# Token product of two batches by seven block products, and the last weights rounded from the pair before the last

## The chip, the cores and the metric

The kernel runs on one core of one Trainium2 chip. The metric is the device time of one execution in microseconds (us). The core's engines run side by side, each with its own queue in order: TensorE (PE) does matrix products out of SBUF into PSUM, VectorE (DVE), ScalarE (ACT) and GpSimd (POOL) do elementwise work, and SyncE (SP) issues the DMA transfers.

## The reference

Two blocks follow each other. The first is an attention in which each query sees only the keys that fall to the same of 16 clusters; the second is a mixer: a small network across the tokens, then one across the channels.

```python
# B, H, S, D = 4, 8, 768, 64; 16 clusters
q_assign = argmax(q_n @ c_n.T); k_assign = argmax(k_n @ c_n.T)     # by batch and head
scores = where(q_assign[:, None] == k_assign[None, :], q @ k.T / 8, -1e9)
x = softmax(scores) @ v                            # bridged to x: (4, 768, 512)

h = relu(x.T @ w_tok1) @ w_tok2                    # 768 -> 256 -> 768 tokens
u = x + h.T
out = u + relu(u @ w_ch1) @ w_ch2                  # 512 -> 1536 -> 512 channels
```

The inputs are random; q, k and v are float32, and the four weights arrive as float64, so the kernel has to round them to float32 itself.

## The kernel before

**Attention.** The loop over `g` runs over 16 pairs of heads (4 batches x 4 pairs). `scores(g, qh)` makes two score tiles per key block, ScalarE takes exponentials (L423), `add_up` sums them on VectorE (L431), `values` multiplies by v (L441), and ScalarE copies the result out (L448). A DMA transpose brings it to token order (`pair_turn`), ScalarE puts it into x (`pair_put`, L466), and VectorE divides by the sums (`pair_out`, L492). Routing for pair g+2 goes beside that.

**Rounding the weights.** `weight_steps` yields one step per piece of at most 512 columns. A step finishes piece i-2 (`rest`: three VectorE operations at L210, L215 and L220, then an integer add on GpSimd at L227), does the ScalarE part of piece i-1 (L203 and L205) and issues the load of piece i on SyncE (L197, 512 KB). The call `rounding(n)` puts n steps at that place of the program order. The first three weights (19 pieces) go into pairs 0 to 14, one or two steps a pair. `w_ch2` (12 pieces) takes the space of the routing tiles and starts in pair 15.

**Token stage.** `tok1(b, t)` is one tile of relu(x^T w_tok1): six accumulated matmuls of 128x512 (L521), and a relu, by turns on VectorE and ScalarE. `tok2(b, j)` is one row block of the second product: two matmuls (L530), and one VectorE add into x (L533). The list `ends` orders them: tok1 of batch b+1 goes ahead of tok2 of batch b. Between them go the rest of the rounding, the sums of the first channel weights (`left_weights`, four VectorE operations over all columns), and `u_steps(0)`, which turns u of batch 0: a ScalarE copy (L591), a DMA transpose (L593) and a ScalarE copy back (L604) for each of eight pieces. `u_sums` then makes four sums of u on VectorE (L544).

**Channel stage.** Both channel products already work with seven block products instead of eight (Strassen in Winograd's form). `chunk` does one chunk of a product in three PSUM tiles X, Z and Y: X takes A11 B11, then S2 T2, S3 T3 and A22 T4 on top; Z takes S1 T1, then S4 B22; Y takes A12 B21. After each product VectorE or ScalarE reads what is in PSUM and adds it to one or another block of the result, while TensorE goes on in another tile. The last product of a chunk is put behind the first one of the next (`late`). The S are sums of the left blocks, the T sums of the right ones. `right_weights` makes the sums of `w_ch2` in the first two chunks.

All engines work in program order; there is no scheduler, the order is as written. PSUM holds eight banks: in the attention six for scores and two for `ps_av`; afterwards two buffers each of X, Z and Y in `ps_m`, and `ps_av`, hardly used.

Of the kernel before, what the change touches and what calls it, by code (L numbers as in the profile page):

```python
# [8 lines left out]
F32 = mybir.dt.float32  # L9
# [10 lines left out]
P = 128  # L20
# [28 lines left out]
def kernel(  # L49
# [131 lines left out]
    def weight_steps(pool, W, names):  # L181
# [8 lines left out]
        def tmp(name, dt, n):  # L190
            bufs = 1 if name == "wT" else 2
            return pool.tile([P, WMAX], dt, tag=name, name=name, bufs=bufs)[:, 0:n]

        def load_bits(src, p):
            n = p["n"] = src.shape[1]
            raw = pool.tile([P, WMAX, 2], U32, tag="raw", name="raw", bufs=3)[:, 0:n]
            nc.sync.dma_start(raw.rearrange("p n two -> p (n two)"), src.bitcast(U32))  # L197
            p["lo"], p["hi"] = raw[:, :, 0], raw[:, :, 1]

        def scalar_part(p):  # L200

            p["h"] = tmp("wh", U32, p["n"])
            nc.scalar.activation(out=p["h"].bitcast(F32), in_=p["hi"].bitcast(F32), func=ACT.Abs)  # L203
            p["up"] = tmp("wup", I32, p["n"])
            nc.scalar.activation(out=p["up"], in_=p["lo"], func=ACT.Copy, scale=float(2.0**-29))  # L205

        def rest(dst, p):
# [11 lines left out]
            T = tmp("wT", U32, p["n"])  # L219
            nc.vector.scalar_tensor_tensor(  # L220
                out=T, in0=p["hi"], scalar=0xC0000000, in1=h,
                op0=ALU.bitwise_and, op1=ALU.bitwise_or,
            )
            T, up = T.bitcast(I32), p["up"]
            if len(dst.shape) == 3:
                T, up = (y.rearrange("t (p j) -> t p j", j=NJ) for y in (T, up))
            nc.gpsimd.tensor_tensor(out=dst.bitcast(I32), in0=T, in1=up, op=ALU.add)  # L227
# [3 lines left out]
        for i in range(len(pieces) + 2):  # L231

            def step(i=i):
                if 2 <= i:
                    rest(pieces[i - 2][0], parts[i - 2])
                if 1 <= i <= len(pieces):
                    scalar_part(parts[i - 1])
                if i < len(pieces):
                    load_bits(pieces[i][1], parts[i])

            yield step
# [259 lines left out]
    turns = [0, 0]  # L501

    def relu(dst, src):
        turns[0] += 1
        if turns[0] % 2:
            nc.vector.tensor_scalar_max(out=dst, in0=src, scalar1=0.0)
        else:
            nc.scalar.activation(out=dst, in_=src, func=ACT.Relu)

    def mtile(shape, name):  # L510
        turns[1] += 1
        return pools["ps_m"].tile(shape, F32, tag="XZ"[turns[1] % 2], name=name)
# [3 lines left out]
    def tok1(b, t):  # L516
# [8 lines left out]
        relu(h1s[b][:, t], pf)  # L525

    def tok2(b, j):
        pu = mtile([P, DM], "pu")
        for t in range(NT):
            nc.tensor.matmul(  # L530
                pu, lhsT=W["tok2"][:, t, j], rhs=h1s[b][:, t], start=(t == 0), stop=(t == NT - 1)
            )
        nc.vector.tensor_tensor(out=xs[b][:, j], in0=pu, in1=xs[b][:, j], op=ALU.add)  # L533
# [12 lines left out]
    def add(dst, a, b):  # L546
        nc.vector.tensor_tensor(out=dst, in0=a, in1=b, op=ALU.add)  # L547

    def left_weights():
# [3 lines left out]
        A = {  # L553
# [6 lines left out]
        yield lambda: add(A["S1"], A["A21"], A["A22"])  # L560
        yield lambda: sub(A["S2"], A["S1"], A["A11"])
        yield lambda: sub(A["A21"], A["A11"], A["A21"])
        yield lambda: sub(A["S4"], A["A12"], A["S2"])
        A["S3"] = A["A21"]
        pools["A"] = A

    def right_weights():

        w = W["ch2"]
        B_ = {  # L570
            f"B{i + 1}{j + 1}": w[:, 6 * i : 6 * i + 6, 256 * j : 256 * j + 256]
            for i in range(2)
            for j in range(2)
        }
        extra = pools["wsums"].tile([P, 3, NCT // 2, DM // 2], F32, name="w2s")
        B_["T1"], B_["T2"], B_["T4"] = (extra[:, i] for i in range(3))
        yield lambda: sub(B_["T1"], B_["B12"], B_["B11"])
        yield lambda: sub(B_["T2"], B_["B22"], B_["T1"])
        yield lambda: sub(B_["B12"], B_["B12"], B_["B22"])
        yield lambda: sub(B_["T4"], B_["B21"], B_["T2"])  # L580
        B_["T3"] = B_["B12"]
        pools["B"] = B_
# [31 lines left out]
    def u_sums():  # L614
        uT = pools["uT"]
        uTs = pools["uTs"] = pools["u"].tile([P, 3, NF // 2, HS], F32, name="uTs")
        R = {"B11": uT[:, 0, 0:2], "B21": uT[:, 0, 2:4], "B22": uT[:, 1, 2:4]}
        R["T1"], R["T2"], R["T4"] = (uTs[:, i] for i in range(3))
        R["T3"] = b12 = uT[:, 1, 0:2]
        sub(R["T1"], b12, R["B11"])  # L620
        sub(R["T2"], R["B22"], R["T1"])
        sub(R["T3"], R["B22"], b12)
        sub(R["T4"], R["B21"], R["T2"])
        pools["R"] = R
# [3 lines left out]
    def chunk(n, product, done, last=False):  # L628


        def ptile(tag):
            return pools["ps_m"].tile([P, n], F32, tag=tag, name="p" + tag)

        X = ptile("X")
# [4 lines left out]
        Z = ptile("Z")  # L639
        product(Z, "S1", "T1", True)  # L640
        done("p5", Z)
        Y = ptile("Y")
# [25 lines left out]
        late.append(end)  # L668

    def ch1_chunk(part, i):  # L670
# [47 lines left out]
        chunk(HS, product, done)  # L718
# [114 lines left out]
    ends = [lambda t=t: tok1(0, t) for t in range(NT)]  # L833
    for b in range(B):
        if b + 1 < B:
            ends += [lambda b=b, t=t: tok1(b + 1, t) for t in range(NT)]
        ends += [lambda b=b, j=j: tok2(b, j) for j in range(NJ)]

# [10 lines left out]
    for g in range(NPAIR):  # L849
        final = g == NPAIR - 1  # L850
        if final:
            assert not weights
            routing.close()
            W["ch2"] = pool("wc2pool", 1, side="right").tile([P, NCT, DM], F32, name="wc2")
            weights = list(weight_steps(stage, W, ("ch2",)))
# [17 lines left out]
        rounding(1)  # L873
        for qh in range(2):
            values(g, qh)
# [11 lines left out]
        rounding(final or g % 2 == 0 and 0 < g < EARLY)  # L887

    ps_sc_stack.close()
    pools["ps_m"] = pool("ps_m", 2, space=PSUM)  # L890
    for m in range(9):
        ends.pop(0)()
        if m == 1:
            pair_put(NPAIR - 1)
            pair_out(NPAIR - 1)
        if m % 3 == 2:
            rounding(2)
    assert not state
    attention.close()
    pools["wsums"] = pool("wsums", 1, side="right")  # L900
    pools["u"] = pool("upool", 1, side="right")
    beside = weights + list(left_weights())
    turning = list(u_steps(0))
    while ends:
        for _ in range(-(-len(beside) // len(ends))):
            beside.pop(0)()
        ends.pop(0)()
        if len(ends) < 18 and turning:
            turning.pop(0)()
    u_sums()  # L910
    staging.close()
    tokens.close()
    pools["mlp"] = pool("mlp", 1)
    beside = list(right_weights())
    for b in range(B):
        for part in range(2):
            for i in range(3):
                ch1_chunk(part, i)
# [5 lines left out]
                for _ in range(2):  # L924
                    if beside:
                        beside.pop(0)()
# [10 lines left out]
            if part == 1 and b + 1 < B:  # L937
                u_sums()
# [217 lines left out]
```

## Time and profile before

| | |
|---|---|
| median of three runs | 844.19 us (844.08 to 844.33) |
| span of the profiled execution | 842.8 us, that run took 844.64 us |
| attention | to 317.7 us |
| token stage | 317.7 to 401.3 us |
| channel stage | from 401.3 us |

The page gives for each engine how long it was busy; in the list of groups a row is one kind of instruction: line, engine, operation, output and inputs, shapes, count, then busy time in all and the mean of one in ns, then how long the engine idled just before such instructions and on whom it waited. In a timeline a row has the start, the length, the instruction, and in brackets the idle time before it and who ended it. Starts are from the beginning of the span. The engine that the end depends on is found in the chain of work that ended last. Records of TensorE overlap: its pace is read from starts.

### The profile page before, as it was taken

What the parts mean: (1) busy time and instruction counts of PE and PEld (TensorE: products, weight loads), DVE (VectorE), ACT (ScalarE), POOL (GpSimd) and SP (SyncE); (2) the same over time, 40 slices, a digit from 0 to 9 for tenths busy, and PEclk for the clock granted to TensorE, in tenths of its full rate; (3) what the DMA queues carried; (4) which work ended last, traced back from release to release, by engine and by line L of the source; (5) the groups of instructions that cost most, each with busy time, mean ns of one, the idle gap of its engine ahead of it and who ended that gap; (6) DMA issues with size and microseconds to landing.
All of it is one profiled execution on the core that took longest, in us unless ns stands there. A gap on an engine that the chain in (4) does not pass through costs nothing.

```text
span 842.8 us, 10776 instructions
## 1 busy us (share of the span) xinstructions
PE 833.5 (99%) x4099; PEld 507.2 (60%) x4099; DVE 501.5 (60%) x846; ACT 374.9 (44%) x571; POOL 45.6 (5%) x40
## 2 busy tenths in 40 slices
PE   9999999999999999999999999999999999999997
PEld 4444444445444444444577686785876867768676
DVE  6879898989898862893653434423454333443342
ACT  5678677777777762453210352103612035220210
POOL 1001010101101000330000000000000000000000
PEclk9999999999999999999999999999999999999999
DMA  8887566867775312541000050000310012200001
GB/s 152 149 162 140 114 138 139 162 131 156 148 136 120 57 44 73 169 99 29 0 1 1 19 107 26 0 1 19 88 45 0 1 19 47 85 1 0 1 16 64
DMA packets 183963, 60.19 MB, mean 71 GB/s; under 512 B 172768, under 2 KB 176864, under 8 KB 183904
## 3 DMA queue, kind: packets, MB, share of 16 engines
q1 hardware_dynamic: 182304, 59.04, 33.3%
q8 instruction: 34, 0.56, 0.3%
q10 hardware_dynamic: 1600, 0.39, 0.2%
q14 instruction: 25, 0.20, 0.1%
HBM read 34.64 MB, written 6.29 MB: 49 GB/s over the span
## 4 chain that ended last, share of the span: by engine, by line
PE 90%; DVE 7%; issue 1%; ACT 0%; DMA 0%; SPq 0%; POOL 0%; DVEq 0%; POOLq 0%
PE sc L416 17%; PE pX L734 15%; PE pX L683 15%; PE av L441 12%; PE pZ L683 7%; PE pZ L734 7%; PE ph L521 4%; PE pY L734 4%; PE pY L683 4%; PE pu L530 3%; DVE sum L431 1%; PE small L477 1%; DVE wh L215 1%; DVE wT L220 1%; PE small L301 1%; DVE wh L210 1%
## 5 line engine op out<-in xcount | busy, mean ns | idle before, releaser
L423 ACT ACTIVATE ex<-sc 128x768 f32<-128x768 f32 x192 | 148.9, 810 | 27.0 <-PE sc L416 15.4
L416 PE MATMUL sc<-qkT 64*128 64x384 f32 x768 | 155.1, 482 | 0.0
L431 DVE TENSOR_TENSOR sum<-sum,ex 128x768 f32<-128x768 f32 x128 | 127.7, 998 | 27.4 <-ACT ex L423 14.7
L441 PE MATMUL av<-ex,va 128*64 128x384 f32 x768 | 127.4, 488 | 0.0
L441 PEld LDWEIGHTS av<-ex,va 128*64 128x64 f32 x768 | 53.8, 137 | 71.7 <-issue 69.0
L416 PEld LDWEIGHTS sc<-qkT 64*128 64x128 f32 x768 | 68.5, 187 | 36.1 <-issue 35.2
L691 ACT COPY p<-pX 128x384 f32<-128x384 f32 x24 | 11.4, 475 | 139.1 <-PE pX L683 120.7
L683 PE MATMUL pX<-uT,wc 128*128 128x384 f32 x192 | 67.4, 487 | 0.0
L416 PE MATMUL sc<-ohT 64*128 64x384 bf16 x384 | 63.3, 324 | 0.3 <-DVE sim L317 0.2
L683 PEld LDWEIGHTS pX<-uT,wc 128*128 128x128 f32 x192 | 36.2, 190 | 24.7 <-issue 1.0
L448 ACT COPY avrows<-av 128x768 uint16<-128x768 uint16 x32 | 25.5, 796 | 47.1 <-PE av L441 47.1
L227 POOL TENSOR_TENSOR wc<-wT,wup 128x512 int32<-128x512 int32 x24 | 33.0, 1375 | 191.4 <-DVE wT L220 191.4
L604 ACT COPY uT<-ucols 128x768 uint16<-128x768 uint16 x32 | 33.7, 1052 | 20.3 <-DMA ucols<-urows 20.3
L521 PE MATMUL ph<-x,wt 128*128 128x512 f32 x96 | 41.9, 594 | 0.8 <-DVE x L533 0.8
L416 PEld LDWEIGHTS <-ohT 64*128 64x128 bf16 x384 | 20.3, 94 | 35.7 <-issue 11.1
L530 PE MATMUL pu<-h,wt 128*128 128x512 f32 x96 | 41.7, 592 | 0.0
L547 DVE TENSOR_TENSOR c<-pZ,u 128x384 f32<-128x384 f32 x24 | 13.4, 558 | 46.8 <-PE pZ L683 46.8
L702 ACT ACTIVATE hA<-hA 128x384 f32<-128x384 f32 x24 | 12.6, 523 | 63.4 <-DVE hA L547 63.4
L547 DVE TENSOR_TENSOR x<-pX,x 128x256 f32<-128x256 f32 x24 | 10.2, 423 | 42.8 <-PE pX L734 42.8
L683 PE MATMUL pZ<-uTs,w1s 128*128 128x384 f32 x96 | 35.0, 487 | 0.4 <-DVE uTs L544 0.4
L734 PE MATMUL pX<-wc,hA 128*128 128x256 f32 x144 | 35.0, 379 | 0.0
L734 PE MATMUL pZ<-w2s,hS 128*128 128x256 f32 x144 | 35.0, 379 | 0.0
(121 smaller groups left out, 1224.0 us busy)
## 6 DMA issues: line engine op xcount, KB each, us to landing
raw<-in_moe_w_ch_dram SPq DMA_DIRECT2D x24, 512.0 KB, 4.3
va<-in_v_dram SPq DMA_DIRECT2D x16, 384.0 KB, 3.7
out_dram<-x SPq DMA_DIRECT2D x24, 256.0 KB, 2.2
qk<-in_k_dram SPq DMA_DIRECT2D x60, 96.0 KB, 3.8
qk<-in_q_dram SPq DMA_DIRECT2D x60, 96.0 KB, 3.4
raw<-in_moe_w_tok_dram SPq DMA_DIRECT2D x3, 512.0 KB, 4.3
raw<-in_moe_w_tok_dram SPq DMA_DIRECT2D x4, 384.0 KB, 3.9
ucols<-urows SPq DMA_TRANSPOSE x32, 2.8
```

The lines of the kernel that those rows point to most:

```text
L227: nc.gpsimd.tensor_tensor(out=dst.bitcast(I32), in0=T, in1=up, op=ALU.add)
L416: nc.tensor.matmul(sc[:, h, 0:HS], lhsT=src[rows, 1, j], rhs=src[rows, 0, js], start=start, stop=not start,)
L423: nc.scalar.activation(out=ex, in_=sc[:, :, 0:HS], func=ACT.Exp, scale=SM_SCALE)
L431: nc.vector.tensor_tensor(out=acc, in0=acc if j > 1 else st["ex", qh, 0], in1=st["ex", qh, j], op=ALU.add)
L441: nc.tensor.matmul(av[h * D : (h + 1) * D], lhsT=st["va"][:, h, j], rhs=ex[:, h], start=(j == 0), stop=(j == NJ - 1),)
L448: nc.scalar.copy(out=st["rows"][:, qh], in_=av.bitcast(U16).rearrange("p (t w) -> p w t", w=2))
L521: nc.tensor.matmul(pf, lhsT=W["tok1"][:, j, t * P : (t + 1) * P], rhs=xs[b][:, j], start=(j == 0), stop=(j == NJ - 1),)
L530: nc.tensor.matmul(pu, lhsT=W["tok2"][:, t, j], rhs=h1s[b][:, t], start=(t == 0), stop=(t == NT - 1))
L547: nc.vector.tensor_tensor(out=dst, in0=a, in1=b, op=ALU.add)
L604: nc.scalar.copy(out=out, in_=pools.pop(("ucols", i)).rearrange("p w j t -> p w (j t)"))
L683: nc.tensor.matmul(psum, lhsT=A[a][:, k, c * P : (c + 1) * P], rhs=R[r][:, k], start=start and k == 0, stop=k == 1, skip_group_check=not s ...
L734: nc.tensor.matmul(psum, lhsT=h2[a][:, k, i * P : (i + 1) * P], rhs=Bw[w][:, 3 * part + k], start=start and k == 0, stop=k == 2, skip_grou ...
```

## The change

The second token product takes two batches at once, side by side as the columns of the right operand, and is made from seven block products. The left operand is `w_tok2` in 2 x 2 blocks (two halves of the hidden index, two halves of the token blocks), the right one the relu tiles `h1s` of batches b and b+1. Each block has three chunks; `tok2_chunks` takes them by turns, three X, three Z and two Y banks at a time, and adds what stands in each bank straight into x after each product, so that an intermediate sum in a bank is added wherever it belongs. `token_weights` and `token_sums` make the S and T. The order is now tok1 of two batches, then 21 products, then the same for the other two.

PSUM: `ps_m` has three buffers each of X and Z; Y takes the two banks of `ps_av`, in the channel stage too. All relus of tok1 go to ScalarE.

Rounding: `rest` works in place in `wh`, the ScalarE part writes over the low words in `raw`, and raw has four buffers and wh three. For `w_ch2` the steps begin in pair 14, load two steps ahead of the ScalarE part (`ahead=2`), and add on VectorE instead of GpSimd. The sums of the first channel weights are made by chunks of 128 columns: chunk 0 in the token stage, chunk c after chunk c-1 of batch 0. Those of the second are made in halves, one for each part of batch 0. `u_sums` comes in two halves, around the last of the token product.

```diff
-    def weight_steps(pool, W, names):
+    def weight_steps(pool, W, names, ahead=1, adder=nc.gpsimd):
...
-            p["up"] = tmp("wup", I32, p["n"])
+            p["up"] = p["lo"].bitcast(I32)
...
-            nc.gpsimd.tensor_tensor(out=dst.bitcast(I32), in0=T, in1=up, op=ALU.add)
+            adder.tensor_tensor(out=dst.bitcast(I32), in0=T, in1=up, op=ALU.add)
...
-        for i in range(len(pieces) + 2):
+        for i in range(len(pieces) + ahead + 1):
...
-    def tok2(b, j):
-        pu = mtile([P, DM], "pu")
-        for t in range(NT):
-            nc.tensor.matmul(
-                pu, lhsT=W["tok2"][:, t, j], rhs=h1s[b][:, t], start=(t == 0), stop=(t == NT - 1)
-            )
-        nc.vector.tensor_tensor(out=xs[b][:, j], in0=pu, in1=xs[b][:, j], op=ALU.add)
...
+    def left_chunk(c):
+        return left_sums(pools["A"], lambda x: x[:, :, c * P : (c + 1) * P])
...
+    def token_sums(b, t):
...
+        if t == 0:
+            sub(R["T1"], R["B12"], R["B11"])
+        else:
+            sub(R["T2"], R["B22"], R["T1"])
+            sub(R["T3"], R["B22"], R["B12"])
+            sub(R["T4"], R["B21"], R["T2"])
...
+    def tok2_chunks(b, half):
...
+        kinds = {
+            "p1": ("X", "A11", "B11", "c11"),
+            "p5": ("Z", "S1", "T1", "c22"),
+            "c11": ("Y", "A12", "B21", "c11"),
+            "u2": ("X", "S2", "T2", "c12"),
+            "c12": ("Z", "S4", "B22", "c12"),
+            "c22": ("X", "S3", "T3", "c22"),
+            "c21": ("X", "A22", "T4", "c21"),
+        }
+
+        def product(name, i):
+            tag, a, r, to = kinds[name]
+            start = name in ("p1", "p5", "c11")
+            if start:
+                banks[tag, i] = ptile(tag, DM)
+            nc.tensor.matmul(
+                banks[tag, i], lhsT=A[a][:, i], rhs=R[r], start=start, stop=True,
+                skip_group_check=not start,
+            )
+            x = xs[b + int(to[2]) - 1][:, HJ * (int(to[1]) - 1) + i]
+            add(x, banks[tag, i], x)
+
+        orders = (
+            (("p1", "012"), ("p5", "012"), ("c11", "01"), ("u2", "012"), ("c12", "01")),
+            (("c22", "012"), ("c12", "2"), ("c11", "2"), ("c21", "012")),
+        )
...
+        if g == NPAIR - 2:
+            assert not weights
+            routing.close()
+            W["ch2"] = pool("wc2pool", 1, side="right").tile([P, NCT, DM], F32, name="wc2")
+            weights = list(weight_steps(stage, W, ("ch2",), 2, nc.vector))
+            rounding(1)
+        rounding(g == NPAIR - 1)
...
+    for b in (0, 2):
+        tok1(b, 0)
+        if b == 0:
+            take(weights, 1)
+            pair_put(NPAIR - 1)
+            pair_out(NPAIR - 1)
...
+            take(list(token_weights()), 4)
+        else:
+            take(turning, 2)
+            take(weights, 2)
+        tok1(b, 1)
+        take(weights, 2)
+        if b == 2:
+            take(turning, 2)
+        tok1(b + 1, 0)
+        token_sums(b, 0)
+        take(weights, len(weights) if b == 2 else 1)
+        if b == 2:
+            left_weights()
+            take(list(left_chunk(0)), 4)
+        tok1(b + 1, 1)
+        token_sums(b, 1)
+        if b == 2:
+            take(turning, len(turning))
+        tok2_chunks(b, 0)
+        if b == 2:
+            u_sums(0)
+        tok2_chunks(b, 1)
+        if b == 0:
+            turning = list(u_steps(0))
...
+                if b == 0:
+                    c = 3 * part + i + 1
+                    for sums_of in left_chunk(c) if c < NCT // 2 else ():
+                        sums_of()
+                    take(others, min(len(others), 2))
```

## The prediction

> **What bounds the kernel now.** I read the page's busy table and 40 slices first, then the chain that ended last, then the groups by form, and last the timelines of TensorE, VectorE, ScalarE and SyncE from 280 to 432 us, where the change acts.
>
> ```profile
> span 842.8 us, 10776 instructions
> ...
> PE 833.5 (99%) x4099; PEld 507.2 (60%) x4099; DVE 501.5 (60%) x846; ACT 374.9 (44%) x571; POOL 45.6 (5%) x40
> ...
> PE   9999999999999999999999999999999999999997
> ...
> DVE  6879898989898862893653434423454333443342
> ...
> PE 90%; DVE 7%; issue 1%; ACT 0%; DMA 0%; SPq 0%; POOL 0%; DVEq 0%; POOLq 0%
> ```
>
> TensorE has work in every slice and holds 90% of the chain. VectorE is near full in the attention (slices 0 to 12) and again in 16 and 17 (337 to 379 us, the token products). A gain has to take TensorE instructions away, or gaps between them. TensorE's timeline of the token stage and its end:
>
> ```profile
> 317.72 20.87 PE L521 MATMUL ph<-x,wt 128*128 128x512 f32 x48
> 338.42 10.46 PE L530 MATMUL pu<-h,wt 128*128 128x512 f32 x24
> 348.72 10.46 PE L521 MATMUL ph<-x,wt 128*128 128x512 f32 x24
> 359.02 10.46 PE L530 MATMUL pu<-h,wt 128*128 128x512 f32 x24
> 370.24 10.57 PE L521 MATMUL ph<-x,wt 128*128 128x512 f32 x24 [0.76 <-DVE x L533]
> 380.65 20.76 PE L530 MATMUL pu<-h,wt 128*128 128x512 f32 x48
> 401.25 1.45 PE L683 MATMUL pX<-uT,wc 128*128 128x384 f32 x4
> 403.06 1.56 PE L683 MATMUL pZ<-uTs,w1s 128*128 128x384 f32 x4 [0.36 <-DVE uTs L544]
> ```
>
> 24 records start 10.30 us apart (338.42 to 348.72), 0.429 us each. A matmul of the program is two records here (96 records for 48 matmuls at L530), so 0.858 us. Gaps: 370.24 - 359.02 is 11.22, 0.92 over 10.30; the next batch is 10.41, 0.11 over; and 401.25 to 404.45 is 3.20 where two groups take 2 x 1.29, 0.62 over.
>
> VectorE's and ScalarE's price list, from the groups by form:
>
> ```profile
> L533 DVE TENSOR_TENSOR x<-pu,x 128x512 f32<-128x512 f32 x24 | 16.3, 687 | 16.9 <-PE pu L530 16.9
> L547 DVE TENSOR_TENSOR x<-pX,x 128x256 f32<-128x256 f32 x24 | 10.2, 423 | 42.8 <-PE pX L734 42.8
> L544 DVE TENSOR_TENSOR uTs<-uT,uTs 128x768 f32<-128x768 f32 x8 | 7.6, 955 | 0.4
> L220 DVE SCALAR_TENSOR_TENSOR wT<-raw,wh 128x512 uint32<-128x512 uint32 x27 | 18.7, 692 | 2.4
> ```
>
> Back to back they start about 0.08 closer than they last (adds of 0.69 start 0.60 apart).
>
> **What the Trainium skill says.** Perfetto Trace Analysis, section "Identifying the Most-Contended Engine": matmul busy time misleads because matmuls are pipelined. The trace agrees: the 128x512 records last 592 ns and start every 429, so I count starts. The same page, "Optimizing Tensor Performance", wants matmul groups to rotate through PSUM banks so that evacuation overlaps; before, L533 keeps pace in the undisturbed stretch (1.02 us idle before each add). VectorE: DVE Perf Modes, "The perf-mode tier table": an fp32 tensor_tensor has only the 1x mode. The rows agree (558 ns for 384 columns, 950 for 768: 1.02 ns a column). GPSIMD Engine Reference, "Key points": GpSimd shares its SBUF interfaces with VectorE. The trace agrees: beside GpSimd's add of 344.47 to 345.79 the bit operation of L215 takes 1.38 us instead of 0.43.
>
> **Part 1, fewer products.** Before: 4 batches x 6 x 2 = 48 matmuls. After: 2 pairs x 7 x 3 = 42. Six matmuls, 12 x 0.429 = 5.15 us, on the path. The gaps of 0.92 and 0.11 come from pieces of rounding and weight sums queued between L533's adds on VectorE, for which tok1 waits; now nothing stands between the 21 adds of the first pair, and tok1 finds banks that were freed long before (three per tag instead of two): -1.03. The gap of 0.62 came from all four u sums standing behind the last token add; two of them now come before those adds: -0.62.
>
> **Part 2, VectorE in the token stage.** It gets 42 PSUM adds of 0.69 instead of 24, 8 sums of h1 (0.69), 4 of the token weights (0.56), the 32-bit add of the rounding (from GpSimd), and loses four relus to ScalarE (0.59, busy 6.2 to 11.0 us in each 21). That add is new on VectorE: as built it runs over 1,024 half-words. Not in the trace; bounds 0.69 (L220, 512 columns) and 1.38 (GpSimd's own); I take 1.2 (1,024 columns at 1.02 ns plus 0.16). One rounded piece then costs VectorE 0.45 + 0.52 + 0.61 + 1.1 = 2.65 us, where with GpSimd beside it pieces started 2.53 apart.
> TensorE should run 317.7, 338.3 (four tok1), 356.3 (21 products, 18.0), 376.9, 394.9.
> First pair: VectorE is free at 314.8 (the end of L492). Seven pieces (18.6), pair_out 1.1, weight sums 2.1, T1 0.6 end about 339.2, when the last relu (338.3 + 0.2 + 0.6) releases T2 to T4; these end at 341.0. TensorE has eight products that need none of them, to 345.2. Adds start at 341.0, 0.60 apart against 0.858 for products, so they catch up by the eighth. Each reuse of a bank lies at least four products after its product. No stall.
> Second pair: ScalarE's relu of tok1(2,0) ends at 362.2, and behind it stand two u copies (0.82), two scalar parts (1.3 each), a relu, and the last two scalar parts, whose loads SyncE issues behind two transposes (1.21 each) and which land about 368.6 and 369.7 (3.7 after issue). Then two uT copies and two u copies (3.7) end at 375.0, and only then tok1(3,0)'s relu. T1 at 376.3; the last piece, four chunk sums (0.43) and T2 to T4 end about 382.2. The first second-operand product starts at 383.8: enough. After the 13th add (390.1) VectorE does T1 and T2 of u (1.9), for which the last uT copy is there at about 390; the add that frees X for A22*T4 ends at 392.7, TensorE wants it at 392.35. Stall 0.35 (bounds 0 and 2.5).
>
> **Part 3, chunked sums of the first channel weights.** Before, all were done at 381. Now those of chunk c stand on VectorE behind chunk c-1's work, and Z of chunk c needs S1:
>
> ```profile
> 409.81 0.56 DVE L547 TENSOR_TENSOR hA<-pX,p 128x384 f32<-128x384 f32 x1 [0.66 <-PE pX L683]
> 410.29 0.55 DVE L704 SCALAR_TENSOR_TENSOR hS<-c,hA 128x384 f32<-128x384 f32 x1
> 410.96 0.56 DVE L708 SCALAR_TENSOR_TENSOR hS<-c,hA 128x384 f32<-128x384 f32 x1
> 411.55 0.56 DVE L544 TENSOR_TENSOR hS<-hS,hA 128x384 f32<-128x384 f32 x1
> 412.03 1.75 DVE L544 TENSOR_TENSOR w2s<-wc 128x1536 f32<-128x1536 f32 x1
> ```
>
> S1 (256 columns, 0.43) would take the place of the row at 412.03 and end at 412.46; with 0.05 to the release, Z starts at 412.51 instead of 412.19, and 0.11 of refill as at 403.06: 0.43. It recurs for chunks 1, 2, 4 and 5 (chunk 3 has second-layer products ahead): +1.7. Bounds 0.8 and 3. The halved sums of the second weights (eight of 0.95 for four of 1.75) fit in the rest: 7.5 us of VectorE work beside 9.03 of TensorE per chunk. These in turn delay h2's S4 and A11 as the two of 1.75 do now.
>
> **Part 4, rounding a pair sooner.** Five loads of 512 KB issue before the token stage, where DMA moved nothing from 307 to 317; on SyncE the load of piece 4 waits for piece 0's rounding to about 317.5, ahead of pair 15's transpose, whose rows are ready at 317.85, so that moves 0.5 us and pair_put, due after 323, does not see it. The scalar parts of pieces 0 to 2 (1.3 each) go into pairs 14 and 15: ScalarE had 0.90 idle before its first exponential and 0.55 at the tenth, and three score buffers bridge the rest. VectorE's pieces 0 and 1 fill its idle 3.03 us before 317.85 and push the last transpose to 320.7, needed by 322.9. All at nothing. In the earlier pairs GpSimd reads its second operand with a stride of 8 bytes and writes as before: bounds 0 and 0.25 us more beside VectorE, for six full pairs 1.5; also the VectorE wait for GpSimd's last piece (2.4 idle in all at L220) goes. Value 0.
>
> Sum against the span of 842.8: -5.15 -1.03 -0.62 +0.35 +1.7 = -4.75, so 838.05. The three times of before (median 844.19) are taken from outside that span, 1.4 above it, so the forecast is 844.19 - 4.75 = 839.4.
>
> **Rivals.**
> 1. The waits of part 3 don't happen and the second pair has none: VectorE reaches S1 early. 839.4 - 2.05 = 837.4. Against: the row at 412.03 is back to back. Chance 0.10.
> 2. VectorE becomes the bound in the second pair and in the chunks: the upper bounds, 2.5 instead of 0.35 and 3 instead of 1.7, give 842.9; two thirds of that excess, 841.7, is its middle. For: 20.53 of 21.65 us busy at 359 to 380. Against: its adds are 0.26 quicker than a product. Chance 0.10.
> 3. The gain is cancelled by the attention: GpSimd's strided add holds VectorE longer, L291's transposes come late (TensorE waited 0.5 for one already), and 16 pairs x 0.3 take 4.8: 844.2. Against: in 11 of 16 pairs VectorE idles before L481, waiting for TensorE. Chance 0.08.
> 4. Slower: the 32-bit add on VectorE. In the first pair seven pieces and 6.3 of other work must pass between 314.8 and 345.2, that is 3.44 a piece, an add of 2.0 us. Beyond it TensorE waits seven times the excess; at 2.7 the gain is gone, at 3.0 the time is 839.4 + 7.1 = 846.5. Chance 0.07.
>
> **How the numbers follow.** The forecast has 0.65 (838.2 to 841.0 by its own bounds). 0.2% is 1.7 us, about what a measurement of this kernel can tell from no change. Faster, under 842.5: forecast, rivals 1 and 2, 0.85; same, rival 3: 0.08; slower, rival 4: 0.07. The range from 837.0 to 842.9 holds the first three.
>
> **What would show it.** 84 records of products, 0.429 apart, the channel stage starting near 395; L710 with a wait under 1 us; pZ of the first layer waiting for w1s about 0.4 us four times; the 32-bit add at 1.2 us; pairs still 19.1 us. Wrong if the add exceeds 2 us, if T1 or T2 of the second pair comes after 383.8, or if the attention ends later than 317.7.

## The result, and the profile after

The changed kernel takes 838.84 us (median of six runs, 838.40 to 838.99) where the kernel before takes 844.32 (six runs beside them, 844.08 to 844.58). The ratio is 0.9935, with a 95% interval from 0.9922 to 0.9947. The forecast was 839.4. The spans of the two profiled executions are 842.8 and 837.0, a difference of 5.8.

These lines of the page of the kernel after answer to those shown of before:

```profile
span 837.0 us, 10822 instructions
...
PE 827.9 (99%) x4087; PEld 502.6 (60%) x4087; DVE 518.4 (62%) x908; ACT 377.3 (45%) x575; POOL 30.7 (4%) x28
...
DVE  6879898989898878759644735424354234443342
...
PE 93%; DVE 5%; issue 0%; DMA 0%; ACT 0%; SPq 0%; DVEq 0%; ACTq 0%
```

TensorE lost 12 records (4099 to 4087) and VectorE took on 62 instructions and 16.9 us, yet VectorE's share of the chain fell from 7% to 5%: what it took on lies mostly beside products. TensorE's timeline of the kernel after, from the token stage on (start, length, and in brackets the wait ahead of the row):

```profile
316.56 20.87 PE L518 MATMUL ph<-x,wt 128*128 128x512 f32 x48
337.26 2.74 PE L710 MATMUL pX<-h,wt 128*128 128x512 f32 x6
...
355.29 20.76 PE L518 MATMUL ph<-x,wt 128*128 128x512 f32 x48
375.89 2.74 PE L710 MATMUL pX<-h,wt 128*128 128x512 f32 x6
...
391.67 2.84 PE L710 MATMUL pX<-h1s,wt 128*128 128x512 f32 x6 [0.17 <-DVE x L536]
394.75 1.53 PE L741 MATMUL pX<-uT,wc 128*128 128x384 f32 x4 [0.24 <-DVE x L536]
396.11 1.45 PE L741 MATMUL pZ<-uTs,w1s 128*128 128x384 f32 x4
...
403.85 1.45 PE L741 MATMUL pX<-uTs,wc 128*128 128x384 f32 x4
405.45 1.56 PE L741 MATMUL pZ<-uTs,w1s 128*128 128x384 f32 x4
```

The 21 products of the first pair take 355.29 - 337.26 = 18.03, which is 42 x 0.429 with no gap at all. Those of the second take 394.75 - 375.89 = 18.86: 0.83 of waits, in two places. Four groups of the channel stage start 1.29 apart when nothing holds them; from 403.85 to 405.45 are 1.60. The starts cut the span into three stretches:

| stretch | before | after | difference |
|---|---|---|---|
| start to the first product of the token stage | 317.72 | 316.56 | -1.16 |
| token stage, to the first product of the channel stage | 83.53 | 78.19 | -5.34 |
| channel stage, to the end | 441.55 | 442.25 | +0.70 |
| span | 842.8 | 837.0 | -5.8 |

The token stage and the channel stage went nearly as forecast. The first row was forecast at 0: the attention, which is not meant to change, became 1.16 shorter. ScalarE's timeline around one pair shows what differs there, in the kernel before:

```profile
183.21 0.80 ACT L448 COPY avrows<-av 128x768 uint16<-128x768 uint16 x1 [2.69 <-PE av L441]
184.33 0.68 ACT L203 ACTIVATE wh<-raw 128x512 f32<-128x512 f32 x1 [0.32 <-DVE wT L220]
185.74 0.68 ACT L205 ACTIVATE wup<-raw 128x512 int32<-128x512 uint32 x1 [0.74 <-POOL wc L227]
186.32 3.59 ACT L423 ACTIVATE ex<-sc 128x768 f32<-128x768 f32 x5
```

and in the kernel after:

```profile
182.74 0.80 ACT L446 COPY avrows<-av 128x768 uint16<-128x768 uint16 x1 [2.68 <-PE av L439]
183.43 0.70 ACT L202 ACTIVATE wh<-raw 128x512 f32<-128x512 f32 x1
184.02 0.68 ACT L204 ACTIVATE raw<-raw 128x512 int32<-128x512 uint32 x1
185.08 4.85 ACT L421 ACTIVATE ex<-sc 128x768 f32<-128x768 f32 x6 [0.38 <-PE sc L414]
```

Before, ScalarE's scalar part stands still twice. The second wait is for GpSimd's add of an earlier piece, which still reads one of the two `wup` buffers. Behind the scalar part stand the exponentials of the next pair, which begin at 186.32, that is 3.11 after the copy of `avrows` began; after, it is 2.34, and they now wait for TensorE instead. There are three score buffers, and the fourth score tile has to wait for the first exponential: before, TensorE starts it at 187.17, where the 0.81 from tile to tile put it at 186.96. The start of the products L441 or L439 shows it pair by pair. Before they start at 175.20, 194.54, 213.66, 233.00, 252.11 and 271.46: every second pair takes 19.34 or 19.35, the others 19.11 or 19.12. After they start at 174.73, 193.84, 212.96, 232.07, 251.19 and 270.30: all take 19.11 or 19.12.

### The profile page after: what moved, and what is told of

It is laid out like the page before. It is cut to its first block, busy times and chain, and to the rows that moved or that the text cites. A ratio compares the mean times of both kernels' runs of the same rounds, so it can differ in the third digit from the quotient of the medians.

```text
span 837.0 us, 10822 instructions
## 1 busy us (share of the span) xinstructions
PE 827.9 (99%) x4087; PEld 502.6 (60%) x4087; DVE 518.4 (62%) x908; ACT 377.3 (45%) x575; POOL 30.7 (4%) x28
## 4 chain that ended last, share of the span: by engine, by line
PE 93%; DVE 5%; issue 0%; DMA 0%; ACT 0%; SPq 0%; DVEq 0%; ACTq 0%
PE sc L414 17%; PE pX L792 15%; PE pX L741 14%; PE av L439 13%; PE pZ L741 8%; PE pZ L792 7%; PE ph L518 5%; PE pY L792 4%; PE pY L741 4%; PE pX L710 2%; PE small L475 1%; DVE sum L429 1%; PE pZ L710 1%; PE small L299 1%; DVE x L536 1%; PE pY L710 1%
## 5 line engine op out<-in xcount | busy, mean ns | idle before, releaser
L421 ACT ACTIVATE ex<-sc 128x768 f32<-128x768 f32 x192 | 151.0, 812 | 28.5 <-PE sc L414 16.9
L439 PE MATMUL av<-ex,va 128*64 128x384 f32 x768 | 127.4, 488 | 0.0
L439 PEld LDWEIGHTS av<-ex,va 128*64 128x64 f32 x768 | 53.7, 137 | 71.7 <-issue 67.5
L536 DVE TENSOR_TENSOR x<-pX,x 128x512 f32<-128x512 f32 (+1 forms) x48 | 25.8, 553 | 44.3 <-PE pX L792 42.8
L792 PE MATMUL pX<-w2s,hA 128*128 128x256 f32 x144 | 35.0, 379 | 0.0
L792 PE MATMUL pY<-wc,hA 128*128 128x256 f32 x144 | 35.0, 379 | 0.0
```

What stands on the lines that cost most here:

```text
L421: nc.scalar.activation(out=ex, in_=sc[:, :, 0:HS], func=ACT.Exp, scale=SM_SCALE)
L439: nc.tensor.matmul(av[h * D : (h + 1) * D], lhsT=st["va"][:, h, j], rhs=ex[:, h], start=(j == 0), stop=(j == NJ - 1),)
L792: nc.tensor.matmul(psum, lhsT=h2[a][:, k, i * P : (i + 1) * P], rhs=Bw[w][:, 3 * part + k], start=start and k == 0, stop=k == 2, skip_grou ...
```

## The experiments

Each kernel is timed against runs of the kernel before on the same chip (medians 844.41, 844.27 and 844.3 in the three sets). These medians differ by 0.14, so differences of that size between kernels of different sets mean nothing.

| kernel | median us | ratio to before, 95% interval | span |
|---|---|---|---|
| after | 838.84 | 0.9935 [0.9922, 0.9947] | 837.0 |
| E1: before with the new rounding buffers | 842.96 | 0.9984 [0.9977, 0.9991] | 841.1 |
| E2: after with the old rounding buffers | 840.11 | 0.9949 [0.9933, 0.9966] | 838.3 |
| E3: after with eight products | 843.18 | 0.9986 [0.9979, 0.9993] | 841.2 |
| E4: after, u sums behind the token adds | 838.66 | 0.9932 [0.9915, 0.9949] | 836.8 |
| E5: after, chunk 0 earlier | 838.97 | 0.9935 [0.9919, 0.9952] | 837.2 |
| E6: after, all six chunks earlier | 837.10 | 0.9914 [0.9897, 0.993] | 835.3 |
| E7: after, 32-bit add on GpSimd | 839.01 | 0.9937 [0.9921, 0.9954] | 837.1 |
| E8: after, two more operations a piece | 843.26 | 0.9989 [0.9982, 0.9995] | 841.3 |
| E9: E6 and E10 together | 835.94 | 0.9901 [0.9886, 0.9916] | 834.5 |
| E10: after, one u sum behind the token adds | 837.87 | 0.9924 [0.9911, 0.9938] | 836.0 |

### E1 and E2: do the rounding buffers explain the attention?

E1 is the kernel before with the in-place buffers alone; GpSimd still adds, the token product has eight products.

```diff
-            bufs = 1 if name == "wT" else 2
-            return pool.tile([P, WMAX], dt, tag=name, name=name, bufs=bufs)[:, 0:n]
+            return pool.tile([P, WMAX], dt, tag=name, name=name, bufs=3)[:, 0:n]
...
-            raw = pool.tile([P, WMAX, 2], U32, tag="raw", name="raw", bufs=3)[:, 0:n]
+            raw = pool.tile([P, WMAX, 2], U32, tag="raw", name="raw", bufs=4)[:, 0:n]
...
-            p["up"] = tmp("wup", I32, p["n"])
+            p["up"] = p["lo"].bitcast(I32)
...
-            T = tmp("wT", U32, p["n"])
...
-                out=T, in0=p["hi"], scalar=0xC0000000, in1=h,
+                out=h, in0=p["hi"], scalar=0xC0000000, in1=h,
```

> The kernel before with only the new buffers of the rounding: work in place in wh, the ScalarE part over the low words of raw, raw four buffers deep and wh three. Theory A: the attention's unforeseen 1.0 us comes from ScalarE no longer waiting for GpSimd's add before the second scalar part of a step, so the first exponential of every other pair is not late. Then all pairs last 19.11 us on TensorE, the token stage starts about 1.0 us sooner (316.7 instead of 317.7), and the time is 843.1 to 843.4. Rival: the 1.0 us belongs to the other order of the rounding or to the start of the run; then it stays at 844.2.

E2 is the reverse of this edit in the kernel after: the same lines, exchanged.

> The kernel after with the old buffers of the rounding (separate tiles for the ScalarE part and the merged word, raw three deep, wh two). Theory A: the six late pairs come back, +0.9 to +1.1 us before the token stage, about 839.8; and since the loads of the last weights then wait one piece longer, up to 0.5 more in the token stage. Rival: no change, 838.8, if the buffers are not what the attention gained from.

TensorE's timeline of E1, the first product of the token stage:

```profile
316.47 20.87 PE L519 MATMUL ph<-x,wt 128*128 128x512 f32 x48
```

and of E2, two pairs and the token stage:

```profile
175.18 7.96 PE L441 MATMUL av<-ex,va 128*64 128x384 f32 x48
194.51 7.96 PE L441 MATMUL av<-ex,va 128*64 128x384 f32 x48
...
317.68 20.87 PE L520 MATMUL ph<-x,wt 128*128 128x512 f32 x48
```

With the new buffers the token stage of the kernel before begins at 316.47 (317.72 without them); with the old ones that of the kernel after begins at 317.68 (316.56), and its pairs take 19.33 again (175.18 to 194.51). So the buffers alone carry the first stretch, in both directions. ScalarE's waits from 20 to 317 us (total, times, longest) point to the buffer. In E2:

```profile
ACT wh L203 <- DVE wT L220: 4.3, 5, 3.1
ACT wup L205 <- POOL wc L227: 2.2, 3, 0.7
ACT wup L205 <- POOL wt L227: 1.8, 3, 0.7
```

The two rows of `wup` stand in the kernel before with the same numbers; neither E1 nor the kernel after has a row of `wup` or of `wh`. The wait for `wh` lasts 0.3 at most before and 3.1 in E2, but the attention is as long in both, so the row of 4.3 costs nothing there. That the buffer is `wup` is read from these rows: E1 and E2 exchange all the buffers together, and no run exchanged `wup` alone.

Not every such wait costs time. The four of 0.72 to 0.74 are each followed by a pair that is 0.16 to 0.24 longer than in the kernel after, those of 0.58 and 0.47 by a pair of the usual length; one more pair, whose end is the start at 175.20, is 0.10 longer, and its cause stays open. From the first product of the attention to the token stage the old buffers take 296.62 (before) and 296.61 (E2), the new ones 295.67 in both the kernel after and E1: 0.95 is the buffers' share. The other 0.21 of the 1.16 is a later start of that first product, 21.10 against 20.89; in the kernels with the new buffers it lies anywhere from 20.70 to 21.05, so this part is not counted as the change's. In time, E2 stands 1.27 above the kernel after. E1 stands 1.45 below its own runs of before. Its span is 1.7 shorter: 1.25 by the attention, and 0.45 in the token stage, where its wait at 368.55 is 0.31 and that of before at 370.24 was 0.76.

### E3: what the missing products are worth

```diff
+        c = b + half
+        for j in range(NJ):
+            pu = ptile("XZ"[j % 2], DM)
+            for t in range(NT):
+                nc.tensor.matmul(
+                    pu, lhsT=W["tok2"][:, t, j], rhs=h1s[c][:, t], start=(t == 0), stop=(t == NT - 1)
+                )
+            add(xs[c][:, j], pu, xs[c][:, j])
...
-            take(list(token_weights()), 4)
...
-        token_sums(b, 0)
...
-        token_sums(b, 1)
```

The seven products, their chunks and their sums of weights and of h1 are gone; all else is as in the kernel after.

> The kernel after, but each batch's second token product is made as before from two matmuls a block (96 records instead of 84), in the new place and the new banks, without the sums of the token weights and of h1. Theory: the seven products are worth 12 records x 0.429 = 5.15 us; without the sums and with 24 adds instead of 42 the waits of the second pair (0.8) go, so 838.8 + 5.15 - 0.8 = 843.2. Rival: the order and the banks are what saved time, and the products only pay for their own waits: 839 to 841.

TensorE's timeline of E3:

```profile
337.18 1.88 PE L696 MATMUL pX<-h,wt 128*128 128x512 f32 x4
...
357.78 20.76 PE L518 MATMUL ph<-x,wt 128*128 128x512 f32 x48
...
398.98 1.45 PE L714 MATMUL pX<-uT,wc 128*128 128x384 f32 x4
```

The products of a pair take 357.78 - 337.18 = 20.60 where the seven take 18.03: 2.57 for each pair, which is 6 x 0.429. E3 has no waits in the second pair, and it takes 4.34 longer than the kernel after: 5.15 less the 0.83 of waits that the seven products bring. The price of what the seven products add on VectorE is thus these 0.83 and little more. The rival, 839 to 841, falls. From 337.18 to 398.98 E3 has no gap at all, so the 1.03 of gaps of the kernel before went with the rest of the change and not with the seven products.

### E4, E5 and E10: the waits of the second pair

E4 moves both u sums of `u_sums(0)` behind the last token adds. E10 moves only the second of them, T2, from `u_sums(0)` to `u_sums(1)`.

```diff
+        tok2_chunks(b, 1)
         if b == 2:
             u_sums(0)
-        tok2_chunks(b, 1)
```

> The kernel after with the first half of the u sums put behind all token adds of the second pair. Theory: the waits of 0.33 at 391.67 and 0.5 at 394.75 come from the adds that stand behind these two sums on VectorE; they go, but Z of the first channel chunk then waits for T1 and T2 behind the last adds, as before the change (0.6). Net -0.2, between 838.4 and 839.0, and TensorE's X of A22*T4 starts 2.57 after the X of S3*T3 plus Z and Y, without a wait. Rival: the waits come from the backlog of the chunk sums and the last piece of rounding alone and stay, so that the new wait comes on top: 839.4.

```diff
-            sub(R["T2"], R["B22"], R["T1"])
         else:
...
+            sub(R["T2"], R["B22"], R["T1"])
```

> The kernel after with only T2 of the u sums moved behind the last token add. Theory B: its two waits in the second pair (0.33 and 0.5) go, and no wait for T1 comes in their place (unlike the run with both sums late): 838.0 to 838.2. Rival: with the chunk sums still ahead of T2 to T4 VectorE is behind anyway, and half of it stays: 838.5.

E5 leaves the u sums where they are and moves the chunk sums of the first channel weights forward, so that VectorE has less to do later.

```diff
-            take(weights, 2)
+            take(weights, 1)
+            left_weights()
+            take(list(left_chunk(0)), 4)
+            take(weights, 1)
...
-            left_weights()
-            take(list(left_chunk(0)), 4)
```

> The kernel after with only the sums of chunk 0 of the first channel weights moved from ahead of T2 to T4 of the second pair into VectorE's idle 4.9 us after the first rounded piece (358.4 to 363.3). Theory: T2 to T4 and all adds of the second pair come 1.4 us sooner, the add that frees X for A22*T4 is there before TensorE wants it, and the waits of 0.33 and 0.5 us go: 838.0. The four waits for S1 in the channel stage stay. Rival: the last uT copy (388.4) and the two u sums set the waits; then at most 0.3 is gained.

TensorE in E4 has lost both waits, and has the wait of the kernel before again:

```profile
394.07 1.45 PE L741 MATMUL pX<-uT,wc 128*128 128x384 f32 x4
395.88 1.56 PE L741 MATMUL pZ<-uTs,w1s 128*128 128x384 f32 x4 [0.36 <-DVE uTs L533]
```

The channel stage begins 0.68 sooner, and 0.84 sooner if one counts from the start of the token stage, which is at 316.72 here. Its first two groups take 3.21 where those of the kernel after take 2.65, so 0.56 is given back. Over two undisturbed groups this is 0.63, the 0.62 of the kernel before: that gap belongs to the place of the u sums. The difference of 0.18 in time agrees, but is too small to be shown by the times. TensorE in E10 has neither:

```profile
391.27 2.74 PE L710 MATMUL pX<-h1s,wt 128*128 128x512 f32 x6
393.85 1.45 PE L741 MATMUL pX<-uT,wc 128*128 128x384 f32 x4
395.13 1.45 PE L741 MATMUL pZ<-uTs,w1s 128*128 128x384 f32 x4
```

It takes 837.87, 0.97 less than the kernel after; the waits of 0.83 and the 0.07 behind them make 0.90. One u sum fits ahead of the last adds without a wait, and one behind them is done in time for Z.

E5 missed its expectation, and its trace shows why it does not decide about the theory. VectorE reached the first token add of the second pair at 379.49 instead of 381.23, yet TensorE's products of that pair take 19.18, more than the 18.86 of the kernel after, and the time is that of the kernel after. VectorE's timeline in E5:

```profile
387.78 0.95 DVE L533 TENSOR_TENSOR uTs<-uT 128x768 f32<-128x768 f32 x1
390.29 0.96 DVE L533 TENSOR_TENSOR uTs<-uT,uTs 128x768 f32<-128x768 f32 x1 [1.56 <-ACT uT L625]
```

and ScalarE's in E5, up to the copy that it waits for:

```profile
384.68 1.05 ACT L625 COPY uT<-ucols 128x768 uint16<-128x768 uint16 x1 [1.83 <-DMA ucols<-urows]
385.60 0.82 ACT L612 COPY urows<-x 128x768 uint16<-128x768 uint16 x1
...
389.21 1.05 ACT L625 COPY uT<-ucols 128x768 uint16<-128x768 uint16 x1 [1.84 <-DMA ucols<-urows]
```

In the kernel after the last two of these copies, and T2 on VectorE, are:

```profile
383.74 0.82 ACT L612 COPY urows<-x 128x768 uint16<-128x768 uint16 x1
...
387.37 1.06 ACT L625 COPY uT<-ucols 128x768 uint16<-128x768 uint16 x1 [0.59 <-DMA ucols<-urows]
...
390.05 0.96 DVE L533 TENSOR_TENSOR uTs<-uT,uTs 128x768 f32<-128x768 f32 x1
```

In E5 VectorE stands idle for 1.56 at T2, while the adds queued behind it hold the banks that TensorE wants. T1 is not held up, because the last transposed piece isn't among those it reads. In the kernel after the last copy ends at 388.43, and VectorE comes to T2 at 390.05, by its own work: there VectorE's backlog sets T2, as E5's theory has it. In E5 it could have begun T2 at about 388.7, but the copies were late. The last transpose itself took 2.8 from issue to landing in both kernels. The late one is the sixth of the eight, which landed after 4.7 instead of 2.8; it held up the copy at 384.68, and the last piece went out 1.86 later than in the kernel after (385.60 against 383.74).

The transfers recorded in the traces show what it met. In E5, 17 of its 800 packets start only at 383.16, 0.95 after the others. That is when a single transfer of 16 KB, on the queue that the profile calls `instruction`, ends (382.30 to 383.18). In the kernel after that transfer starts at 382.87, and all 800 packets had passed by 382.30. In E6 and E9 the two meet as in E5: 17 packets are late there too, and the transpose lands after 4.2. No run moved that transfer on purpose, so this is a reading of traces. Without the meeting E5's adds would have followed T2 from about 389.6 (an estimate from the rows above), as early as in E10, where they start at 389.65 and no wait is left. Whether the other three runs of E5 met it too isn't recorded; all four times, 838.38 to 839.29, lie above the 838.0 expected.

E10 takes T2 out of the way of these adds, whichever chain is late: VectorE's own in the kernel after, that of the transposes and copies in E5 and E6.

### E6: the chunk sums out of the channel stage

All six chunks of the sums of the first channel weights are made in the token stage, in VectorE's idle time there.

```diff
+            for c in (0, 2, 3):
+                take(list(left_chunk(c)), 4)
...
+            for c in (4, 5):
+                take(list(left_chunk(c)), 4)
...
+        else:
+            take(list(left_chunk(1)), 4)
...
-                    c = 3 * part + i + 1
-                    for sums_of in left_chunk(c) if c < NCT // 2 else ():
-                        sums_of()
```

> The kernel after with the sums of all six chunks of the first channel weights in VectorE's idle times of the token stage: chunk 1 ahead of T2 of the first pair, 0, 2 and 3 after piece 7, 4 and 5 after piece 10. Theory: the four waits for S1 of 0.42 us in the channel stage and the two of the second pair go, 0.84 + 1.7 = 2.5: 836.3. Rival: something else stands right behind in the chunks (h2's sums, the sums of the second weights), so the Z of chunks 1, 2, 4 and 5 wait anyway: 838.0; or VectorE now holds T1 of the second pair: over 838.

In the kernel after, VectorE's timeline has S1 of chunk 1 behind the work of chunk 0:

```profile
404.50 0.56 DVE L533 TENSOR_TENSOR hS<-hS,hA 128x384 f32<-128x384 f32 x1
404.98 0.42 DVE L536 TENSOR_TENSOR w1s<-wc 128x256 f32<-128x256 f32 x1
```

S1 ends at 405.40, and Z starts at 405.45. TensorE's timeline in E6:

```profile
403.78 1.45 PE L741 MATMUL pX<-uTs,wc 128*128 128x384 f32 x4
405.07 1.45 PE L741 MATMUL pZ<-uTs,w1s 128*128 128x384 f32 x4
```

Here Z follows in 1.29. The time falls by 1.74; the four chunks, 0.41 to 0.48 each, make 1.72. The expected 836.3 is missed by 0.8, because one of the second pair's two waits remains: the channel stage's first X comes at 394.68, 0.5 late. VectorE is early enough here, but T2 waits 1.03 for the last uT copy, after the late transpose described above.

### E7 and E8: is VectorE's load in the token stage near a bound?

E7 gives the 32-bit add of the last weights back to GpSimd.

```diff
-            weights = list(weight_steps(stage, W, ("ch2",), 2, nc.vector))
+            weights = list(weight_steps(stage, W, ("ch2",), 2, nc.gpsimd))
```

> The kernel after with the integer add of the last weights on GpSimd instead of VectorE. Theory: a piece costs VectorE 2.35 us with its own add (0.69); with GpSimd's add beside it the next piece's first operations take 0.9 longer, so VectorE's load is the same within 0.2 us a piece and hidden: 838.5 to 839.3. Rival: the move to VectorE was needed for the second pair: its waits grow by over 1 us, 840 or more.

E8 does an operation of VectorE three times for each of these pieces; a second and third time change nothing in its result.

```diff
-            nc.vector.scalar_tensor_tensor(
-                out=h, in0=p["hi"], scalar=0xC0000000, in1=h,
-                op0=ALU.bitwise_and, op1=ALU.bitwise_or,
-            )
+            for _ in range(3 if adder is nc.vector else 1):
+                nc.vector.scalar_tensor_tensor(
+                    out=h, in0=p["hi"], scalar=0xC0000000, in1=h,
+                    op0=ALU.bitwise_and, op1=ALU.bitwise_or,
+                )
```

> The kernel after with one operation of each rounded piece of the last weights done three times (it gives the same words again): 1.45 us more on VectorE a piece. Theory: in the first pair VectorE idles 3.8 us after piece 0 and TensorE's first product with T2 starts 3.5 after it could, 7.2 us of room for seven pieces, 1.03 each. 7 x 1.45 = 10.2 is 2.9 too much: a wait of about 3 us before the product S2*T2 of the first pair, none or under 1 us more in the second: 841.5 to 842.5. Rival: VectorE's load is far from the path: no change, 838.8; or the room is not there, since the idle times are waits for ScalarE that don't shrink: 7 us more, over 845.

E7 takes 839.01, the same as the kernel after: the add is hidden on either engine. It is not free on GpSimd, though. VectorE's timeline in E7:

```profile
315.38 1.51 DVE L214 TENSOR_SCALAR wh<-wh 128x512 uint32<-128x512 uint32 x1
...
329.92 1.39 DVE L214 TENSOR_SCALAR wh<-wh 128x512 uint32<-128x512 uint32 x1
```

In the kernel after this operation lasts 0.43. In four of the twelve pieces it meets an add on GpSimd and is stretched by 0.96 to 1.08, more than the 0.69 that VectorE is rid of; in a fifth it is L209 that is stretched, by 0.61. In all, L214 takes 759 ns in the mean of 12 pieces instead of 427 and L209 472 instead of 416, 4.7 us of the 8.3 that the twelve adds took.

E8 takes 843.26. TensorE's timeline in its first pair:

```profile
337.14 2.74 PE L711 MATMUL pX<-h,wt 128*128 128x512 f32 x6
340.46 2.84 PE L711 MATMUL pZ<-h1s,wt2s 128*128 128x512 f32 x6 [0.58 <-DVE h1s L534]
...
346.57 2.84 PE L711 MATMUL pX<-h1s,wt2s 128*128 128x512 f32 x6 [1.55 <-DVE x L537]
...
358.31 20.76 PE L519 MATMUL ph<-x,wt 128*128 128x512 f32 x48
```

The first pair's products take 358.31 - 337.14 = 21.17, 3.14 over 18.03, and the second pair's 20.10, 1.24 over the 18.86 of the kernel after. The wait that the fourth rival spoke of is real. A piece costs VectorE 2.35 in the kernel after, from start to start, and with 1.45 more 3.80 here; the rival put the limit at 3.44, and seven times the excess is 2.5. The wait does not lie at T2, as the expectation had it, but at T1 (0.75 ahead of S1*T1, the row at 340.46) and at the first bank to be used again (1.71 ahead of the row at 346.57, whose bank is freed by an add that stands behind T2 to T4 on VectorE). The kernel after is clear of it, with no wait in the first pair. The time is 0.8 above the upper end of my expectation: the second pair lost more than I had allowed.

### E9: both improvements

E9 has the edits of E6 and of E10.

> The kernel with all six chunks' sums early (the run before), and of the u sums only T1 ahead of the second half of the products, T2 behind the last add. Theory B, formed since: in the second pair the adds behind T2 wait for the last uT copy, that is for the chain of copies and DMA transposes on ScalarE, and not for VectorE's backlog; T1 needs only the first six of the eight pieces. So no add waits for ScalarE, the waits of 0.1 and 0.5 us before the channel stage go, and T2 (behind the last add, about 395.5) is in time for S2*T2 at 397.9: 837.1 - 0.6 = 836.5. Rival: the wait at 394.7 belongs to the bank itself and stays, 837.1; or S2*T2 now waits, over 837.1.

TensorE's timeline in E9:

```profile
391.48 2.74 PE L710 MATMUL pX<-h1s,wt 128*128 128x512 f32 x6
394.05 1.45 PE L741 MATMUL pX<-uT,wc 128*128 128x384 f32 x4
395.34 1.45 PE L741 MATMUL pZ<-uTs,w1s 128*128 128x384 f32 x4
...
404.37 1.45 PE L741 MATMUL pZ<-uTs,w1s 128*128 128x384 f32 x4
```

No wait is left from the last products to Z of the second chunk. It takes 835.94, 2.90 less than the kernel after (2.5 in the spans; the profiled execution was the slowest of its four), where E6 saved 1.74 and E10 0.97. It is the fastest of all, at 0.9901 of the kernel before. Theory B of the expectation holds for E6, from which it was formed; in the kernel after T2 waits for VectorE's backlog, not for ScalarE. The sixth transpose is late in E9 too, 4.2, and TensorE does not notice it, since no add stands behind T2.

## Why the prediction was right, point by point

| step of the forecast | forecast us | measured us | by what |
|---|---|---|---|
| part 1, six matmuls fewer | -5.15 | -5.15 | E3, 2.57 a pair |
| part 1, gaps of 0.92 and 0.11 | -1.03 | -1.03 | starts, none left in the first pair, none in E3 either |
| part 1, Z waits for the u sums | -0.62 | -0.62 | no such wait at 396.11; E4 has it again, 0.63 |
| part 2, waits of the second pair | +0.35 | +0.90 | 18.86 less 18.03, and 0.07 behind; E10 |
| part 3, Z waits for S1, four chunks | +1.7 | +1.7 | 0.41, 0.42, 0.48, 0.41; E6, 1.74 |
| small gaps of the channel stage before | not counted | -0.42 | starts at 417.49 and 426.72 |
| part 4, the attention | 0 | -1.16 | E1 and E2: 0.95; the other 0.21 is not the change's |

The small gaps were four: 0.14 and 0.10 ahead of products of the channel stage of before at 417.49 and 426.72, and 0.10 and 0.08 in the groups that follow. The kernel after has none there, and I had not counted them. The measured terms come to -5.76, the difference of the spans within rounding.

- **The products and their gaps** came out as worked out. All 84 records are 0.429 apart where nothing waits. The banks in turn gave no wait in the first pair: VectorE's adds began at 339.91 (forecast 341.0 with a start 1.16 later) and had caught up by the eighth, at 344.33, where VectorE waits for TensorE for the first time. One sum of the forecast is off: its list of VectorE's work in the first pair, from 314.8, ends at 337.2 and not at 339.2. It changed nothing, since T2 was to wait for the last relu at 339.1, as it does (2.21, to 338.09).
- **The 32-bit add** was mis-sized: 1.2 us was taken, between 0.69 and 1.38, and it lasts 0.692, its lower bound. Its group in the kernel after, by form:

```profile
L225 DVE CUSTOM_DVE_ANT_0 wc<-raw,wh 128x1024 uint16<-128x1024 uint16 x12 | 8.3, 692 | 1.1
```

It costs nothing in time (E7), and the forecast had it hidden at 1.2 too. VectorE: DVE Perf Modes, section "The perf-mode tier table", gives a tensor_tensor over 16-bit bf16 values in SBUF twice the pace of fp32. I took the fp32 pace for 1,024 columns; the row shows 1,024 half-words in the time of 512 words (L218, 693 ns). The table does not list this operation, so that it runs in that mode is an inference from the number.
- **The waits of the second pair** were placed rightly and half sized. The forecast had one wait of 0.35, ahead of A22*T4; it is there, 391.67 instead of 391.34, 0.33. It missed the second: the channel stage's first X takes the bank of the first A22*T4, whose add is as late as the others, because VectorE gains only 0.26 on TensorE with each add. It starts at 394.75 instead of 394.25, and 0.07 more is lost in that group (1.36 to the next instead of 1.29).
- **The S1 waits** were forecast at 0.43 each from the row that S1 would take the place of, and measured 0.41 to 0.48 (from 403.85, the next group but one starts at 406.84, 2.99 later where two groups take 2.58).
- **The attention** is the step that failed. Part 4 put it at 0 and looked for a loss of up to 1.5. It asked what GpSimd's strided add does to VectorE, and noted that a wait of VectorE goes; it did not ask who else waits for GpSimd. The rows of `wup` in ScalarE's waits (2.2 and 1.8 us, six times) stood in the trace of before, and behind each stand a pair's exponentials. With the new buffers, `wup` among them in raw, the rows are gone, and 0.95 us with them.

Of the rivals, the first (no S1 waits and none in the second pair) is what E9 makes true by moving the sums, and gives 835.94 where it said 837.4, without the attention and the small gaps. The second did not happen: VectorE kept below its bound. The third went the other way: the pairs became shorter. The fourth needs an add of 2 us; E8 brings a piece to that load and shows the wait, 3.14 in the first pair.

The forecast left out gains of 1.16 in the attention and 0.42 in small gaps, and a loss of 0.55 in the second pair. So its sum, -4.75, falls short of the spans' difference by 1.0, and of the 5.48 between the medians by 0.7. The main term, the six matmuls, came out as worked out; that the omissions partly cancel is luck.

## What to carry to other kernels

When a change gives a buffer more copies, or lets an engine write in place, look in the profile at the waits of every engine that writes that buffer, not just of the one whose work the change concerns. A row of a few tenths that recurs can cost part of its time where the work queued behind it feeds the bound: here six waits of 4.0 in all went together with 0.95. When a product fills a bank that an engine empties, follow the chain of banks past the end of the stage, since the next stage's first product takes the bank of the last add. Where two chains end at one instruction, a run that shortens one of them (E5) can show nothing because the other came late that time; look at what the instruction waited for before the theory is given up, and move the instruction out of the way (E10, E9).

## What the runs showed of the hardware

- The add of two 32-bit integers on VectorE, built as an operation on half-words, takes 0.692 us for 128 x 512, with the second operand read at a stride of 8 bytes.
- GPSIMD Engine Reference, section "Key points", says that GpSimd shares its SBUF interfaces with VectorE. E7 gives the size here: an operation of 0.43 us on VectorE takes 1.39 to 1.51 beside an add on GpSimd that lasts 1.28 to 1.35, so it is held for most of that. Over the twelve pieces of the last weights more than half of the time that VectorE is spared comes back in this way.
- A transpose by DMA of one piece of u of batch 0 lands 2.8 us after its issue in the kernel after, all eight times. In the profiled executions of E5, E6 and E9 one of the eight takes 4.7, 4.2 and 4.2: 17 of its 800 packets start only when a 16 KB transfer of 0.88 us on the `instruction` queue ends. In E5 and E6 this put T2 back by 1.56 and 1.03, and with it the adds that free TensorE's banks.
